# Attention, gated MLP and channel mixer on one core: VectorE's part of the last spatial weights in a step of its own, and the constants of the next stage behind the attention

## Chip, core and metric

The kernel runs on one core of a Trainium2 chip. The metric is the device time of one execution in microseconds (us); the median of three runs is given. Engines are named as the profile names them: PE (TensorE), DVE (VectorE), ACT (ScalarE), POOL (GpSimd), SP (SyncE, which only issues DMAs here).

## What is computed

Three layers follow one another; batch 8, 8 heads, 576 tokens, head size 64.

```python
# 1: attention with features (128 + 128 per token)
proj = q @ w_phi;  proj -= max(abs(proj));  phi = concat(exp(proj), exp(-proj))
kv = phi(k).T @ v;  z = phi(k).sum(tokens)
x  = (phi(q) @ kv) / (phi(q) @ z + 1e-6)
# 2: gated MLP over tokens
h = relu(x @ w_in);  u, v = halves(h)
v_n = (v - mean(v)) / sqrt(var(v) + 1e-6)
v_s = w_spatial @ v_n + b_spatial[:, None]
x = (u * v_s) @ w_out
# 3: low rank over tokens, then a channel MLP
u = x + V.T @ (U.T @ x);   out = u + relu(u @ w_ch1) @ w_ch2
```

Matmul operands of layers 2 and 3 are split into a high and a low part (`hi = round(w)`, `lo = w - hi`), and products use both.

## The kernel before

**Attention.** `attention` walks over 32 pairs of heads with a software pipeline, one period of the loop variable `p` for each (p from -1 to 34, the last ones draining). In period p PE projects the keys and queries of pair p+1 into one PSUM tile `pa` (line 402, tiles pk and pq), transposes the queries of p (pt, line 434), sums key times value of p and p+1 (pkv, lines 468 and 475), and makes the outputs of pairs p-2 and p-1 in four groups (pn, line 503), all with tag "pn" or "kv", one buffer each. DVE takes the largest value of a projection (mk and mq, line 411) and subtracts it (sk and sq, line 414); only then is `pa` free for the next projection. ACT makes the exponentials (kp, qp, e), POOL the low part of qp (line 456, two instructions for each e). An output group leaves PSUM by a copy to `nd`: on ACT (line 514), or on DVE for group 1 (line 512), and until that copy is done PE can't start the next group in the same buffer. These instructions are pinned: they keep the order in which the code writes them.

**Side work.** Between them `step(work)` runs one step of a side job at four places of a period: behind the subtraction sk ("slot 1"), behind kp ("slot 2"), between qp and e ("slot 3"), and at the period's end ("slot 4", called with `last=True`), ahead of the DVE copy `nd` of group 1. A step marked `late` runs at slot 4 alone. `with self.behind()` puts a step behind the latest pinned instruction of each engine. A job fetches weights, repacks and splits them; the next job begins when the last one is done. Side jobs share one staging buffer, tag "w32". The jobs in order: 16 pieces of `w_in`, four `w_sp` (rows of the spatial weights), `w_sp_tail` (the last 64 rows, and the bias in the free rows of the same tile `wt1`), 8 pieces of `w_out` (half a piece of 512 columns each; `raw_wo`, `bits_wo`, `w32_wo`), each four slots long. In `w_sp_tail` the step `bias` copies the 64 rows on ACT (line 212), subtracts on DVE (line 213), clears the staging tile for the bias on DVE (line 217) and issues its two DMAs on SP (line 220); the step `bias_split` makes two copies on ACT (line 228) and a subtraction on DVE (line 229). Both steps are late.

**Next stage.** `alloc_moe` (lines 636 to 651) runs once behind the attention's code: it allocates the tiles of layer 2 and writes the rows of constants for the bias, `vn1`, over a staging tile `pad` (DVE, lines 648 to 651). These instructions aren't pinned, and the scheduler of the framework may move them to an earlier place on their engine. Then `values(0, t)` for five tiles of tokens, t = 0 to 4: PE makes pv, ACT (DVE for the last) puts relu into v, DVE makes mean and variance (`bn_stats`, `bn_aggr`, lines 731 and 732), POOL the power -0.5 (rstd, line 734), DVE normalizes (line 739) and casts to vn0, POOL subtracts for vn1 (line 135). The normalization of tile t is written behind the statistics' matmuls of t+1. `gate(0)` follows: pu (two passes for each of four column blocks), then pz. PE's PSUM tiles have four buffers, so pu of the second block waits until the pv tile of t = 4 has been read (line 725). Meanwhile the attention's last divisions (x, POOL line 549, behind a DMA `rec`) are still under way.

Of the kernel before, what the change touches and what calls it, by code (L numbers as in the profile page):

```python
# [93 lines left out]
class Mixer:  # L94
# [69 lines left out]
    def weight_jobs(self):  # L164


        nc, jobs = self.nc, []
        S, R, NF, tail = self.S, self.R, self.NF, self.tail
# [34 lines left out]
        def w_sp_tail():  # L203


            wt0, wt1 = self.wt[0][:, NF, :], self.wt[1][:, NF, :]
            w = self.stage("wt", S)
            for i in range(2):
                nc.sync.dma_start(w[i * tail : (i + 1) * tail, :], self.w_spT[NF * P :, :])

            def bias():
                nc.scalar.copy(wt0, w)
                nc.vector.tensor_tensor(
                    out=wt1[:tail, :], in0=w[:tail, :], in1=wt0[:tail, :], op=ALU.subtract
                )
                b = self.stage("bs", S)
                nc.vector.memset(b[tail:, :], 0.0)
                for i in range(2):
                    r = tail + i * 32
                    nc.sync.dma_start(b[r : r + 1, :], self.b_sp)  # L220
                f = lambda: bias_split(b)
                f.late = True
                return f

            def bias_split(b):
                for i in range(2):
                    r = slice(tail + i * 32, tail + (i + 1) * 32)
                    nc.scalar.copy(wt1[r, :], b[r, :])
                nc.vector.tensor_tensor(
                    out=wt1[r, :], in0=b[r, :], in1=wt1[r, :], op=ALU.subtract  # L230
                )

            bias.late = True
            return bias

        jobs.append(w_sp_tail)
        def w_out(kk, h):
            def f():
# [397 lines left out]
    def alloc_moe(self, left, right):  # L636
        tc, nc, NF, tail = self.tc, self.nc, self.NF, self.tail
        self.ps = self.ctx.enter_context(
            tc.tile_pool(name="ps", bufs=1, space=PSUM, reuse_waits="tile")
        )  # L640
        mp = self.mp = left.enter_context(tc.tile_pool(name="mp", bufs=1, reuse_waits="tile"))
        self.gs = self.gated(0)
        mq = self.mq = right.enter_context(tc.tile_pool(name="mq", bufs=1, side="right", reuse_waits="tile"))


        self.vn = [mq.tile([P, self.NST, self.DH], F32R, name=f"vn{i}") for i in range(2)]
        pad = self.stage("pad", self.DH)
        nc.vector.memset(pad[tail:, :], 0.0)
        for r in (tail, tail + 32):
            nc.vector.memset(pad[r : r + 1, :], 1.0)  # L650
        nc.vector.tensor_copy(self.vn[1][tail:, NF, :], pad[tail:, :])

    def gated(self, b):
        return self.mp.tile([P, 2, self.KH, self.S], F32R, tag="g", name=f"g_{b}", bufs=1)
# [448 lines left out]
```

## Time and profile before

| | us |
|---|---|
| median of 3 runs | 1706.85 (1704.88 to 1708.28) |
| the profiled execution | 1698.59 |
| its span, first to last instruction | 1696.8 |
| what lies around the span | 1.8 |
| PE busy in the span | 1649.7 (97%) |
| attention, up to the first matmul of values(0, 0) | 387.9 |

A row of the timeline reads: start in us, length in us, engine, line, operation, output<-input, shapes, count of instructions merged into the row, and in brackets the idle time of the engine just before it and who ended it. A table by windows has one row for each stretch.

### The profile page before, as it was taken

How to read it: one execution, taken by the hardware profiler on the slowest of the kernel's cores; microseconds unless marked ns; L12 is line 12 of the kernel's file. 1: busy time of each engine (PE TensorE's matmuls, PEld its weight loads, DVE VectorE, ACT ScalarE, POOL GpSimd, SP SyncE). 2: the span in 40 equal slices, each digit the busy share in tenths (PEclk: the TensorE clock that was granted, in tenths of full speed). 3: DMA queues.
4: the chain of work that ended last, by engine and by line, in shares of the span. 5: the costliest groups of instructions: out<-in, count | busy, mean ns of one | idle time of the engine just before them, and what ended most of it. 6: DMA issues, size and time to landing. Idle time of an engine off the chain costs nothing.

```text
span 1696.8 us, 26606 instructions
## 1 busy us (share of the span) xinstructions
PE 1649.7 (97%) x10824; PEld 1559.9 (92%) x10824; DVE 741.5 (44%) x1234; ACT 609.4 (36%) x1092; POOL 470.4 (28%) x402
## 2 busy tenths in 40 slices
PE   7999989989999999999999999999999999999999
PEld 7998978978889789889789999999999999999999
DVE  6888766855656766656647112112111021121120
ACT  5888757863344443344334012011021120110110
POOL 3777775755333334224221000000000000000000
PEclk9999999999999999999999999999999999999999
DMA  4677665742233342232235101101001011011000
GB/s 136 196 199 212 203 189 145 197 124 71 79 121 98 117 122 87 91 109 82 70 101 164 38 1 37 38 1 38 21 18 38 1 38 38 1 38 38 1 19 20
DMA packets 86143, 141.42 MB, mean 83 GB/s; under 512 B 18626, under 2 KB 41314, under 8 KB 86020
## 3 DMA queue, kind: packets, MB, share of 16 engines
q1 hardware_dynamic: 85876, 139.65, 27.7%
q8 instruction: 85, 1.39, 0.3%
q14 instruction: 38, 0.31, 0.1%
q10 hardware_dynamic: 144, 0.07, 0.0%
HBM read 93.25 MB, written 36.85 MB: 77 GB/s over the span
## 4 chain that ended last, share of the span: by engine, by line
PE 78%; DMA 9%; DVE 4%; ACT 4%; issue 2%; POOL 2%; SPq 1%; DVEq 0%; POOLq 0%; ACTq 0%
PE pc L662 24%; PE ph L662 23%; DMA raw_c<-in_w_ch 5%; PE pu L662 4%; PE pn L503 4%; PE pv L662 4%; PE pkv L475 4%; PE px L662 4%; PE pz L662 2%; PE pk L402 1%; PE pt L434 1%; PE pt L867 1%; PE pq L402 1%; PE py L871 1%; DMA den<-nd 1%
## 5 line engine op out<-in xcount | busy, mean ns | idle before, releaser
L662 PE MATMUL pc<-h,w 128*128 128x384 f32 x2304 | 403.8, 336 | 0.0
L662 PEld LDWEIGHTS pc<-h,w 128*128 128x128 f32 x2304 | 402.0, 188 | 0.0
L662 PE MATMUL ph<-us,w 128*128 128x384 f32 x2244 | 391.0, 334 | 0.0
L662 PEld LDWEIGHTS ph<-us,w 128*128 128x128 f32 x2244 | 389.2, 188 | 0.0
L915 ACT ACTIVATE h<-ph 128x384 fp32r<-128x384 f32 x187 | 92.0, 492 | 628.5 <-PE ph L662 626.2
L135 POOL TENSOR_TENSOR us<-u,us 128x384 fp32r<-128x384 f32 x48 | 48.6, 1041 | 682.9 <-ACT us L132 673.9
L916 DVE SCALAR_TENSOR_TENSOR h<-ph,h 128x384 fp32r<-128x384 f32 x187 | 104.3, 558 | 273.1 <-ACT h L915 273.0
L503 PE MATMUL pn<-qp,kv 128*65 128x288 f32 x768 | 210.8, 335 | 13.0 <-DVE nd L512 9.7
L456 POOL TENSOR_TENSOR qp<-e,qp 128x576 fp32r<-128x576 f32 x128 | 184.1, 1460 | 132.3 <-ACT e L453 102.2
L951 DVE TENSOR_TENSOR u<-pc,u 128x384 f32<-128x384 f32 x48 | 25.7, 558 | 363.4 <-PE pc L662 363.4
L475 PE MATMUL pkv<-v,kp 128*128 128x65 f32 x1024 | 156.2, 256 | 0.0
L475 PEld LDWEIGHTS pkv<-v,kp 128*128 128x128 f32 x1024 | 155.4, 196 | 0.0
L503 PEld LDWEIGHTS pn<-qp,kv 128*65 128x65 f32 x768 | 101.4, 143 | 19.3 <-DVE nd L512 11.7
L662 PE MATMUL pz<-wt,vn 128*128 128x288 f32 x768 | 112.2, 295 | 0.0
L662 PEld LDWEIGHTS pu<-xs,wi 128*128 128x128 f32 x768 | 104.3, 191 | 3.2 <-DVE v L725 2.5
L662 PE MATMUL pu<-xs,wi 128*128 128x288 f32 x768 | 104.9, 298 | 2.3 <-DVE v L725 2.3
L662 PEld LDWEIGHTS pz<-wt,vn 128*128 128x128 f32 x768 | 105.3, 188 | 0.3 <-DVE u L808 0.3
L662 PE MATMUL px<-wo,g 128*128 128x512 f32 x384 | 93.9, 403 | 10.5 <-ACT g L132 10.5
L662 PEld LDWEIGHTS px<-wo,g 128*128 128x128 f32 x384 | 73.1, 194 | 29.0 <-ACT g L132 13.2
L662 PE MATMUL pv<-wi,xs 128*128 128x512 f32 x384 | 92.2, 394 | 0.0
L662 PEld LDWEIGHTS pv<-wi,xs 128*128 128x128 f32 x384 | 72.0, 188 | 15.6
L425 ACT ACTIVATE kp<-sk 128x1152 f32<-128x1152 f32 x64 | 74.4, 1164 | 31.2 <-DVE sk L414 23.4
(141 smaller groups left out, 1937.6 us busy)
## 6 DMA issues: line engine op xcount, KB each, us to landing
raw_c<-in_w_ch SPq DMA_DIRECT2D x32, 512.0 KB, 4.3
v<-in_v SPq DMA_DIRECT2D x32, 325.0 KB, 4.3
k<-in_kT SPq DMA_DIRECT2D x32, 320.0 KB, 3.7
q<-in_qT SPq DMA_DIRECT2D x32, 320.0 KB, 4.0
x<-nd SPq DMA_DIRECT2D x64, 144.0 KB, 3.3
rec<-rd SPq DMA_DIRECT2D x64, 144.0 KB, 3.3
xd<-x SPq DMA_DIRECT2D x32, 288.0 KB, 2.4
x<-xd SPq DMA_DIRECT2D x32, 288.0 KB, 3.1
```

Of the source, the lines that this page charges most:

```text
L135: return (nc.gpsimd if elo == "pool" else nc.vector).tensor_tensor(out=lo, in0=src, in1=hi, op=ALU.subtract)
L402: self.pin(nc.tensor.matmul(pa[:, j * NF + t, :], x[d, t * P : (t + 1) * P], ws[d, :], start=True, stop=True,))
L425: self.pin(self.nc.scalar.activation(kp, self.st[p]["sk"], AF.Exp, scale=1.0 - 2.0 * i))
L434: self.pin(nc.tensor.transpose(pt[:, at, :], s[:, u, :], self.ident))
L456: self.pin(nc.gpsimd.tensor_tensor(out=lo[:, c], in0=e[:, c], in1=hi[:, c], op=ALU.subtract))
L475: self.pin(nc.tensor.matmul(pkv[:, i, j, :], kp[:, j * NF + t, :], vb[:, u * D1 : (u + 1) * D1], start=False, stop=(j == 1 and t == NF - 1),))
L503: self.pin(nc.tensor.matmul(pn, kv[k][:, i, g // 2, :], qp[q][:, i, g * HS : (g + 1) * HS], start=(m == 0), stop=(m == len(terms) - 1),))
L662: self.nc.tensor.matmul(out, x, y, start=(start and i == 0), stop=(stop and i == len(terms) - 1))
L867: nc.tensor.transpose(pt[:, s0 - c0 : s0 - c0 + n], ts[t][0][:n, fs], self.ident[:n, :n])
L915: nc.scalar.activation(h[:, 0, :], ph, AF.Relu)
L916: nc.vector.scalar_tensor_tensor(out=h[:, 1, :], in0=ph, scalar=0.0, in1=h[:, 0, :], op0=ALU.max, op1=ALU.subtract,)
L951: nc.vector.tensor_tensor(out=u[:, f, :], in0=pcs[f], in1=u[:, f, :], op=ALU.add)
```

## The change

The job `w_sp_tail` gets two more steps. What was one step (ACT copy and DVE work) is now two: the ACT copies stay at slot 4, as late steps, and the DVE subtraction stands in a step of its own, which isn't late, so that it comes at slot 1 of the following period. The clearing of the bias's staging tile and its two DMAs go with the first of these subtractions. The job is one period longer by that, and all eight `w_out` jobs behind it begin one period later. In `alloc_moe` the four instructions for `pad` and the cast to `vn1` are put behind the attention's pinned instructions.

```diff
+            def late(f):
+                f.late = True
+                return f
+
             def bias():
                 nc.scalar.copy(wt0, w)
+                return less
+
+            def less():
                 nc.vector.tensor_tensor(
                     out=wt1[:tail, :], in0=w[:tail, :], in1=wt0[:tail, :], op=ALU.subtract
                 )
...
-                f = lambda: bias_split(b)
-                f.late = True
-                return f
-
-            def bias_split(b):
+                return late(lambda: bias_parts(b))
+
+            def bias_parts(b):
                 for i in range(2):
                     r = slice(tail + i * 32, tail + (i + 1) * 32)
                     nc.scalar.copy(wt1[r, :], b[r, :])
+                return lambda: bias_less(b, r)
+
+            def bias_less(b, r):
                 nc.vector.tensor_tensor(
                     out=wt1[r, :], in0=b[r, :], in1=wt1[r, :], op=ALU.subtract
                 )
...
-        nc.vector.memset(pad[tail:, :], 0.0)
-        for r in (tail, tail + 32):
-            nc.vector.memset(pad[r : r + 1, :], 1.0)
-        nc.vector.tensor_copy(self.vn[1][tail:, NF, :], pad[tail:, :])
+        with self.behind():
+            nc.vector.memset(pad[tail:, :], 0.0)
+            for r in (tail, tail + 32):
+                nc.vector.memset(pad[r : r + 1, :], 1.0)
+            nc.vector.tensor_copy(self.vn[1][tail:, NF, :], pad[tail:, :])
```

**Place 1: DVE at the end of period 20.** Names carry the pair of heads (sq21 belongs to pair 21); `wt1<-w32_wt,wt0` is the subtraction, `w32_bs` the staging tile of the bias. Before:

```order
L414 TENSOR_TENSOR sq21_3005<-pq21_2983,mq21_3004 128x1152
L213 TENSOR_TENSOR wt1_118<-w32_wt_2916,wt0_117 64x576
L217 MEMSET w32_bs_3043 64x576
L512 TENSOR_SCALAR nd19_3008<-pn19_1_3024,eps_133 65x288
L535 RECIPROCAL den9_18_2974<-den9_18_2974 128x9
L411 TENSOR_REDUCE mk22_3078<-pk22_3055 128x9
```

The same place now:

```order
L422 TENSOR_TENSOR sq21_3005<-pq21_2983,mq21_3004 128x1152
L520 TENSOR_SCALAR nd19_3008<-pn19_1_3024,eps_133 65x288
L543 RECIPROCAL den9_18_2974<-den9_18_2974 128x9
L419 TENSOR_REDUCE mk22_3073<-pk22_3050 128x9
L422 TENSOR_TENSOR sk22_3074<-pk22_3050,mk22_3073 128x1152
L220 TENSOR_TENSOR wt1_118<-w32_wt_2916,wt0_117 64x576
L224 MEMSET w32_bs_3079 64x576
L497 TENSOR_TENSOR kv1_21_3114<-pkv21_3011,kv0_21_3113 128x260
```

The subtraction and the clearing have moved from ahead of nd19 to behind sk22. The subtraction of the bias, line 229, moves in the same way, from ahead of nd20 to behind sk23.

**Place 2: DVE in period 30.** Before:

```order
L411 TENSOR_REDUCE mk31_4335<-pk31_4312 128x9
L648 MEMSET w32_pad_4604 64x512
L414 TENSOR_TENSOR sk31_4336<-pk31_4312,mk31_4335 128x1152
L650 MEMSET w32_pad_4604 1x512 x2
L489 TENSOR_TENSOR kv1_30_4369<-pkv30_4273,kv0_30_4368 128x260
```

Now:

```order
L419 TENSOR_REDUCE mk31_4325<-pk31_4302 128x9
L422 TENSOR_TENSOR sk31_4326<-pk31_4302,mk31_4325 128x1152
L60 TENSOR_SCALAR bits_wo3_1_4354<-raw_wo3_1_4300 128x256
L64 SCALAR_TENSOR_TENSOR bits_wo3_1_4354<-raw_wo3_1_4300,bits_wo3_1_4354 128x256
L68 ISA bits_wo3_1_4354<-bits_wo3_1_4354,low_wo3_1_4330 128x512
L497 TENSOR_TENSOR kv1_30_4365<-pkv30_4260,kv0_30_4364 128x260
```

The clearing of `pad` has left the place ahead of sk31, and the last piece of w_out stands in period 30 instead.

**Place 3: DVE and POOL at the first tile of layer 2's values.** st, mv and rstd are the statistics, v0_0 and v0_1 the tiles t = 0 and 1. DVE now (before, the rows of w32_pad, the cast to vn1 and w32_z stood above the first row, and the cast to vn0 ahead of the second BN_STATS):

```order
L740 BN_STATS st0_0_4627<-v0_0_4610 128x6
L543 RECIPROCAL den9_31_4575<-den9_31_4575 128x9
L657 MEMSET w32_pad_4604 64x512
L741 BN_AGGR mv0_0_4628<-st0_0_4627 128x2
L659 MEMSET w32_pad_4604 1x512 x2
L742 TENSOR_SCALAR rstd0_0_4629<-mv0_0_4628 128x1
L660 CAST vn1_4603<-w32_pad_4604 64x512
L748 TENSOR_SCALAR v0_0_4610<-v0_0_4610,mv0_0_4628,rstd0_0_4629 128x512
L740 BN_STATS st0_1_4652<-v0_1_4635 128x6
L134 CAST vn0_4602<-v0_0_4610 128x512
L741 BN_AGGR mv0_1_4653<-st0_1_4652 128x2
L269 MEMSET w32_z_4766 128x128
```

The constants have moved in between the statistics of t = 0 and their normalization, and each of the first two casts to vn0 behind the next tile's BN_STATS. POOL before:

```order
L734 TENSOR_TENSOR rstd0_0_4629<-rstd0_0_4629,mhalf_105 128x1
L135 TENSOR_TENSOR vn1_4603<-v0_0_4610,vn0_4602 128x512
L549 TENSOR_TENSOR x30_4532<-x30_4532,rec30_4556 128x576
L734 TENSOR_TENSOR rstd0_1_4654<-rstd0_1_4654,mhalf_105 128x1
L135 TENSOR_TENSOR vn1_4603<-v0_1_4635,vn0_4602 128x512
```

POOL now:

```order
L743 TENSOR_TENSOR rstd0_0_4629<-rstd0_0_4629,mhalf_105 128x1
L557 TENSOR_TENSOR x30_4532<-x30_4532,rec30_4556 128x576
L135 TENSOR_TENSOR vn1_4603<-v0_0_4610,vn0_4602 128x512
L743 TENSOR_TENSOR rstd0_1_4654<-rstd0_1_4654,mhalf_105 128x1
L135 TENSOR_TENSOR vn1_4603<-v0_1_4635,vn0_4602 128x512
```

On POOL the division x30, which waits for a DMA, has moved ahead of the first subtraction for vn1.

## Rows read from the trace of the kernel before

**Rows 1.** The page, part 1: busy us (share of span), instructions.
```profile
PE 1649.7 (97%) x10824; PEld 1559.9 (92%) x10824; DVE 741.5 (44%) x1234; ACT 609.4 (36%) x1092; POOL 470.4 (28%) x402
```

**Rows 2.** Timeline of DVE, 200 to 300 us (columns as told above).
```profile
236.93 1.30 DVE L411 TENSOR_REDUCE mk<-pk 128x9 f32<-128x1152 f32 x1
...
241.90 0.43 DVE L489 TENSOR_TENSOR kv<-pkv,kv 128x260 fp32r<-128x260 f32 x1 [2.21 <-ACT kv L488]
...
248.15 1.96 DVE L213 TENSOR_TENSOR wt<-w_wt,wt 64x576 fp32r<-64x576 f32 x1 [2.78 <-ACT wt L212]
250.34 0.54 DVE L217 MEMSET w_bs<- 64x576 f32 x1 [0.23 <-DVE wt L213]
...
251.46 1.29 DVE L411 TENSOR_REDUCE mk<-pk 128x9 f32<-128x1152 f32 x1
...
265.35 1.14 DVE L229 TENSOR_TENSOR wt<-w_bs,wt 32x576 fp32r<-32x576 f32 x1 [3.61 <-ACT wt L228]
...
267.07 1.29 DVE L411 TENSOR_REDUCE mk<-pk 128x9 f32<-128x1152 f32 x1
...
280.65 1.36 DVE L411 TENSOR_REDUCE mk<-pk 128x9 f32<-128x1152 f32 x1 [0.88 <-PE pk L406]
```

**Rows 3.** Timeline of all engines, 246 to 252 us.
```profile
247.44 0.67 ACT L212 CAST wt<-w_wt 128x576 fp32r<-128x576 f32 x1
248.10 3.26 POOL L456 TENSOR_TENSOR qp<-e,qp 128x576 fp32r<-128x576 f32 x2
...
251.48 0.35 PE L503 MATMUL pn<-qp,kv 128*65 128x288 f32 x1 [3.93 <-DVE nd L512]
```

**Rows 4.** Timeline of all engines, 263 to 268 us.
```profile
267.09 0.50 PE L503 MATMUL pn<-qp,kv 128*65 128x288 f32 x1 [3.16 <-DVE nd L512]
```

**Rows 5.** Windows of 2 us: PE, PEld, DVE, ACT, POOL busy; granted clock; DMA; GB/s.
```profile
252.00:254.00 2.00, 2.00 (x14) 2.00 (x12) 1.97 (x2) 0.00 (x0) 0.00 (x0) 0.51 0.40 82
```

**Rows 6.** Timeline of all engines, 355 to 373 us.
```profile
356.71 1.36 DVE L411 TENSOR_REDUCE mk<-pk 128x9 f32<-128x1152 f32 x1 [0.88 <-PE pk L406]
...
361.22 0.48 DVE L648 MEMSET w_pad<- 64x512 f32 x1 [3.15 <-POOL wo L135]
...
363.20 1.16 PE L402 MATMUL pq<-wst,q 64*128 64x128 f32 x16 [2.37 <-issue]
```

**Rows 7.** Timeline of PE, 355 to 440 us.
```profile
355.10 1.16 PE L402 MATMUL pk<-wst,k 64*128 64x128 f32 x16
...
356.43 0.38 PE L503 MATMUL pn<-qp,kv 128*65 128x288 f32 x1
...
372.29 0.35 PE L503 MATMUL pn<-qp,kv 128*65 128x288 f32 x1 [0.61 <-DVE nd L512]
```

**Rows 8.** Timeline of all engines, 390 to 409 us.
```profile
394.50 0.69 DVE L731 BATCH_NORM_STATS2 st<-v 128x6 f32<-128x512 f32 x1
394.67 1.30 POOL L135 TENSOR_TENSOR vn<-v,vn 128x512 fp32r<-128x512 f32 x1 [1.12 <-DVE vn L134]
...
397.46 1.44 POOL L549 TENSOR_TENSOR x<-x,rec 128x576 f32<-128x576 f32 x1 [1.50 <-DMA rec<-rd]
...
399.45 0.55 DVE L739 TENSOR_SCALAR v<-v,mv,rstd 128x512 f32<-128x512 f32 x1 [3.85 <-POOL rstd L734]
...
408.02 1.23 PE L662 MATMUL pu<-xs,wi 128*128 128x288 f32 x7 [2.27 <-DVE v L725]
```

**Rows 9.** Windows of 2 us, columns as in group 5.
```profile
366.00:368.00 2.00, 2.00 (x12) 1.98 (x12) 1.97 (x2) 1.05 (x2) 0.88 (x1) 0.50 0.37 76
...
410.00:412.00 2.00, 2.00 (x10) 2.00 (x10) 1.24 (x4) 0.62 (x2) 0.57 (x2) 0.50 0.00 0
```

**Rows 10.** Timeline of all engines, 236 to 272 us.
```profile
241.00 1.16 PE L402 MATMUL pq<-wst,q 64*128 64x128 f32 x16
...
245.20 0.53 SPq L372 DMA_DIRECT2D q<-in_qT  x1
```

**Rows 11.** The page, part 6: DMA issues, KB each, median us to landing.
```profile
q<-in_qT SPq DMA_DIRECT2D x32, 320.0 KB, 4.0
```

## The prediction

> **What bounds the kernel now.** I read part 1 of the page first: PE is busy 97% of the span [rows 1], so an edit on another engine pays only where PE stands still or runs at half its clock because of it. Then the timeline of DVE by periods of the attention, then the stretches in which a period is long, with all engines, and last the windows with the granted clock. The mark of a period is the start of its mk. Seven periods, from 280.65 to 356.71, take 76.06 us, 10.87 each [rows 2, 6]; PE shows no wait worth a row in them, so 10.87 is the undisturbed length. Three periods ahead of them take 236.93 to 280.65 [rows 2], 43.72 us where 3 x 10.87 = 32.6 would do: **11.1 us too long**, just where the two DVE subtractions of the change stand. A further period, 30, is long where `pad` is cleared.
>
> In the first case ACT makes its copy only at 247.44, behind the last e of the period, and the subtraction waits for it, 2.78 us of idle DVE, then takes 1.96 and the clearing of the bias tile follows with 0.54 [rows 2, 3]. The copy `nd` of group 1 is queued behind both on DVE, and PE needs the buffer that `nd` empties: PE stands still for 3.93 us [rows 3]. In the next period the same happens with the bias (DVE waits 3.61, the subtraction takes 1.14), and PE stands still for 3.16 [rows 2, 4]. That is 7.1 us of the 11.1. The other 4.0 is clock: after the stop the granted clock is 0.51 at 252 to 254 [rows 5], which is the lower level, 1.2 GHz of 2.4, and PE is busy all through that window.
>
> In period 30 the scheduler has put the clearing of `pad` ahead of sk31. It waits 3.15 us for POOL's last subtraction of `w_out`, since both use the one staging buffer [rows 6]. The subtraction sk31 comes late, the PSUM tile `pa` isn't free, and PE's projection pq starts after 2.37 us of idle [rows 6]; then the clock is at 0.50 again [rows 9].
>
> **The change part by part.**
>
> *The two subtractions.* At slot 4 only ACT's copies are left (0.67 us for the first; the second step has two). Neither is new, and `nd` of group 1 is on DVE, no longer behind anything. On DVE the subtraction and the clearing now stand between sk and the split kv of the next period, where DVE was idle for 2.21 us until ACT had copied kv [rows 2]. ACT's result has been there for several us by then, so no wait goes with them. Their price at the old durations is 1.96 + 0.23 + 0.54 = 2.73 us [rows 2], 0.5 more than the idle time; kv could be late by that, and PE's next pkv with it. I charge 0.2, bounds 0 and 0.5. The second subtraction, 1.14, fits. Gain: 11.1 - 0.2.
>
> The row of 1.96 us is long because POOL's pair of subtractions starts 0.05 us ahead of it and takes 3.26 [rows 3]. The Trainium skill (SBUF — State Buffer, Who interferes with whom) says that a VectorE instruction with two SBUF inputs and a GpSimd instruction that reads SBUF take a shared port in turn, for whole instructions; the row looks like that. By this rule the subtraction in its new place meets only the end of such a pair and is shorter, and the sum would be better by the 0.2; by the row alone it stays as charged.
>
> *The shifted job.* `w_sp_tail` ends a period later, so each of the eight `w_out` pieces does too, and the last one fills period 30. The seven undisturbed periods carry such pieces already, so a period with one costs 10.87: nothing added, nothing won. Its DMAs (raw_wo on SP) move with it; the first load of layer 3's U is issued a period later, while its reader comes behind 408. The bias's two DMAs move on SP from ahead of rd to behind v, ahead of den, x and q; see the last rival.
>
> *`pad` in period 30.* PE's groups there begin at 356.43 and the next ones at 372.29: 15.86 us. An undisturbed period is 10.87, but no keys are left to project, which takes off the pk pass, 355.10 to 356.43 = 1.33 [rows 7]; and without that pass PE waits 0.61 for `nd` [rows 7], which stays. So 10.87 - 1.33 + 0.61 = 10.15 is what it should be, and 5.7 us go. Of these 2.37 are the stop, and most of the rest is the clock.
>
> *`pad` in the next stage.* Here something is given back. DVE's clearing, cast and the clearing of z, some 2 us in all, come between the statistics and the normalization of tile 0. That alone costs nothing: tile 1 couldn't be normalized before 399.45, after 3.85 us of idle DVE, because POOL's division x waits for its DMA until 397.46 and rstd is behind it [rows 8]. But the order on POOL changes: x30 now stands ahead of the subtraction for vn1, which takes 1.30 [rows 8] and was done while POOL waited for the DMA. Now it comes between x30 and rstd: +1.30. One tile on, BN_STATS (0.69) stands ahead of the cast for which POOL's subtraction waits [rows 8]: +0.69, as the chain goes back and forth between DVE and POOL with nothing to spare. Both end at the read of the last pv tile, for which PE already waits 2.27 us at 408.02 [rows 8]: **+2.0** there. The bounds: 0, if the DMA comes later than the chain, and 4.1, if after the longer stop the lower clock lasts as long as after period 30's (5.7 - 2.37 - 0.22, the small wait behind it, = 3.1) and not only the 2 us at 0.50, or 1.0 lost, that the windows show at 410 now [rows 9]: 2.0 + 2.1. For the clock I take 0.4.
>
> *Sum.* 11.1 - 0.2 + 5.7 - 2.0 - 0.4 = **14.2 us less**. The profiled execution, 1698.59 with 1.8 around its span, would become 1684.4. It lies 8.3 below the median of the runs, which the trace doesn't explain; I take the same difference off the median: 1706.85 - 14.2 = 1692.6.
>
> **The rivals.**
>
> *More is given back.* PE waits the 0.5 us in period 21 and loses clock by it (4.0 for two stops, so 2.0 for one), and the values stage costs its upper 4.1. Then 16.8 - 2.5 - 4.1 = 10.2: 1696.6. For it: after each of the three stops shown the clock fell [rows 5, 9]. Against: 0.5 us is far shorter than these stops of 2.3 us and more, and kv needn't be late at all.
>
> *Nothing is given back.* The chain of the values ends with POOL's wait for the DMA of x31 anyway, or BN_STATS hides. Then 16.8, and 1.0 more if the clock holds: 1689.0 to 1690.0. Against: the DMA that POOL waited for had landed by 397.46, and both additions lie behind that [rows 8].
>
> *The stop moves instead of going.* The change may not do what it says, if what holds PE at the end of periods 20 and 21 is ACT's copies, not the DVE work behind them: they stay at slot 4. Then the 11.1 remain and only 5.7 - 2.4 = 3.3 go: 1703.5. Against: the bracket of PE's wait names nd on DVE both times [rows 3, 4], and ACT has nothing to do with that buffer.
>
> *Slower.* SP works in order, and the bias's DMAs, which wait for the clearing on DVE, now stand ahead of q, whose staging buffer is single. q is issued at 245.20, 8.27 into its period, and lands 4.0 later [rows 2, 10, 11]; the pq pass that reads it comes 10.87 + 4.07 = 14.94 in (241.00 is 4.07 in) [rows 10], so there is 2.7 us of slack. If the clearing were later than SP by more than that, PE would wait for q, with everything behind it. Subtraction and clearing can start when sk is done, 2.8 into the period (DVE falls idle 2.21 ahead of 241.90 [rows 2]), and be done at 2.8 + 2.73 = 5.5, and q itself is issued 8.27 in, so SP meets no wait; to be slower by 3.4 the hold has to be 2.7 + 14.2 + 3.4 = 20 us, nearly two periods, at one place: 1710.
>
> **How the numbers follow.** My forecast, 11 to 16.5 us less, gets 0.70; more given back 0.13; nothing given back 0.08; the stop that moves 0.06; slower 0.03. The likeliest gives 1692.6. The range takes in the first two rivals with half a microsecond to two for the scatter of the runs (they spread 1.7 around the median), and leaves out the last two: 1687.5 to 1698.0. A measurement of this kernel can tell about 0.2%, 3.4 us, from no change. Faster by more: 0.70 + 0.13 + 0.08 and a little of the fourth, 0.92; within: 0.05; slower: 0.03.
>
> **What would show it.** In the timeline of the changed kernel: mk to mk near 10.87 in periods 20 to 22, no PE wait for nd of 3 us, and a clock of 1.0 through them; the subtraction of the 64 rows directly behind sk, with no idle ahead of it; in period 30 sk31 behind mk31 at once and pq without a wait; at pu in the values stage a PE wait of about 4.3 us on line 734's read of the last pv tile, where it was 2.27. I am wrong if PE's waits in periods 20 to 22 are only renamed, if a new wait for kv or q stands in period 21, or if PE's wait in the values stage is above 7 us.

## The result and the profile after

The changed kernel takes 1689.26 us (median of 6 runs, 1685.94 to 1693.13); the kernel before, in runs beside it, 1705.87 (6 runs, 1695.98 to 1716.75). The ratio is 0.9912, interval 0.9886 to 0.9937: 0.9% faster, 15 us. A second set, with 17 runs of the kernel before, gave 0.9899 (0.9874 to 0.9924). The prediction was 1692.6 in a range of 1687.5 to 1698.0.

The profiled execution of the changed kernel has a span of 1686.3, 10.5 below that of before. To see where it went I cut the spans at five marks: the start of the mk of period 20, three periods on, the mk of period 30, the first pv matmul of layer 2 and the first pz matmul. All numbers are differences of start times in the timelines; the last row ends with the span. A 0 stands where the prediction has no term.

| stretch, us | before | changed | changed, 2nd profile | predicted change |
|---|---|---|---|---|
| start to mk of period 20 | 236.9 | 240.2 | 244.0 | 0 |
| periods 20 to 22 | 43.7 | 32.6 | 32.6 | -10.9 |
| periods 23 to 29 | 76.1 | 76.6 | 76.3 | 0 |
| mk of period 30 to first pv | 31.2 | 25.5 | 25.3 | -5.7 |
| first pv to first pz | 29.7 | 32.5 | 31.5 | +2.4 |
| first pz to the end | 1279.2 | 1279.0 | 1278.1 | 0 |

The three periods first: DVE's timeline of the changed kernel, the rows that answer to [rows 2]. DVE instructions in order of time; start, length, idle time ahead in brackets.

```profile
251.81 1.30 DVE L419 TENSOR_REDUCE mk<-pk 128x9 f32<-128x1152 f32 x1
253.22 1.36 DVE L422 TENSOR_TENSOR sk<-pk,mk 128x1152 f32<-128x1152 f32 x1
254.49 0.74 DVE L220 TENSOR_TENSOR wt<-w_wt,wt 64x576 fp32r<-64x576 f32 x1
255.47 0.54 DVE L224 MEMSET w_bs<- 64x576 f32 x1 [0.23 <-PE pn L511]
256.45 0.43 DVE L497 TENSOR_TENSOR kv<-pkv,kv 128x260 fp32r<-128x260 f32 x1 [0.45 <-ACT kv L496]
...
262.08 1.36 DVE L419 TENSOR_REDUCE mk<-pk 128x9 f32<-128x1152 f32 x1 [0.33 <-PE pk L414]
...
264.93 1.14 DVE L237 TENSOR_TENSOR wt<-w_bs,wt 32x576 fp32r<-32x576 f32 x1
267.04 0.43 DVE L497 TENSOR_TENSOR kv<-pkv,kv 128x260 fp32r<-128x260 f32 x1 [0.96 <-ACT kv L496]
...
272.72 1.36 DVE L419 TENSOR_REDUCE mk<-pk 128x9 f32<-128x1152 f32 x1 [0.88 <-PE pk L414]
```

Both subtractions start as soon as sk is done, with no idle time in their brackets, and kv still waits a little for ACT behind them: nothing is late by them. The two PE waits of 3.93 and 3.16 us [rows 3, 4] have no row any more, and the granted clock is 1.00 in every window of 2 us from 238 to 276 us. The first subtraction takes 0.74 us, where it took 1.96 beside POOL's pair [rows 3]; in this kernel that pair is over at 254.36 us, 0.13 ahead of it.

Period 30, on the timelines of DVE and PE, the rows that answer to [rows 6]:

```profile
349.34 1.36 DVE L419 TENSOR_REDUCE mk<-pk 128x9 f32<-128x1152 f32 x1 [0.88 <-PE pk L414]
350.80 1.36 DVE L422 TENSOR_TENSOR sk<-pk,mk 128x1152 f32<-128x1152 f32 x1
```

```profile
353.40 1.16 PE L410 MATMUL pq<-wst,q 64*128 64x128 f32 x16
```

sk31 follows mk31 at once, and pq starts without a wait.

What was given back stands at the first tile of the values. Timeline of POOL, changed kernel, the rows that answer to [rows 8]:

```profile
381.78 0.70 POOL L743 TENSOR_TENSOR rstd<-rstd,mhalf 128x1 f32<-128x1 f32 x1 [1.87 <-DVE rstd L742]
384.29 1.43 POOL L557 TENSOR_TENSOR x<-x,rec 128x576 f32<-128x576 f32 x1 [1.81 <-DMA rec<-rd]
385.67 1.30 POOL L135 TENSOR_TENSOR vn<-v,vn 128x512 fp32r<-128x512 f32 x1
386.93 0.56 POOL L743 TENSOR_TENSOR rstd<-rstd,mhalf 128x1 f32<-128x1 f32 x1
389.08 1.29 POOL L135 TENSOR_TENSOR vn<-v,vn 128x512 fp32r<-128x512 f32 x1 [1.59 <-DVE vn L134]
```

The subtraction for vn1 (1.30) now stands between x and the rstd of the second tile. The end of that chain, PE's wait for the read of the last pv tile, and the clock behind it (windows of 2 us; the column ahead of the DMA share is the granted clock):

```profile
396.53 1.81 PE L671 MATMUL pu<-xs,wi 128*128 128x288 f32 x6 [3.92 <-DVE v L734]
```

```profile
394.00:396.00 2.00, 0.00 (x0) 0.00 (x0) 1.97 (x3) 0.00 (x0) 1.18 (x2) 0.94 0.00 1
396.00:398.00 2.00, 1.47 (x6) 1.47 (x7) 1.93 (x3) 0.00 (x0) 1.24 (x1) 0.50 0.37 146
398.00:400.00 2.00, 2.00 (x10) 2.00 (x9) 1.18 (x5) 0.18 (x1) 0.54 (x1) 0.50 0.00 0
400.00:402.00 2.00, 2.00 (x11) 2.00 (x10) 1.97 (x4) 0.44 (x2) 1.33 (x1) 0.50 0.00 0
402.00:404.00 2.00, 2.00 (x15) 2.00 (x15) 0.81 (x3) 0.62 (x2) 0.00 (x0) 0.85 0.03 8
```

PE waits 3.92 us instead of 2.27, and the clock is at its lower level for some 6 us of PE's work behind it. In the second profile PE waits 4.14 us.

### The profile page after: what moved, and what is told of

It is laid out like the page before. It is cut to its first block, busy times and chain, and to the rows that moved or that the text cites. A ratio compares the mean times of both kernels' runs of the same rounds, so it can differ in the third digit from the quotient of the medians.

```text
span 1686.3 us, 26604 instructions
## 1 busy us (share of the span) xinstructions
PE 1643.5 (97%) x10824; PEld 1554.4 (92%) x10824; DVE 742.6 (44%) x1234; ACT 609.7 (36%) x1092; POOL 469.0 (28%) x402
## 4 chain that ended last, share of the span: by engine, by line
PE 79%; DMA 9%; ACT 4%; DVE 4%; POOL 2%; issue 2%; SPq 1%; POOLq 0%; ACTq 0%; DVEq 0%
PE pc L671 24%; PE ph L671 23%; DMA raw_c<-in_w_ch 5%; PE pn L511 4%; PE pu L671 4%; PE pv L671 4%; PE pkv L483 4%; PE px L671 4%; PE pk L410 2%; PE pz L671 2%; PE pt L442 1%; PE pt L876 1%; PE pq L410 1%; PE py L880 1%; DMA den<-nd 1%
## 5 line engine op out<-in xcount | busy, mean ns | idle before, releaser
L671 PE MATMUL px<-wo,g 128*128 128x512 f32 x384 | 93.6, 401 | 11.1 <-ACT g L132 11.1
```

The lines of the kernel that those rows point to most:

```text
L671: self.nc.tensor.matmul(out, x, y, start=(start and i == 0), stop=(stop and i == len(terms) - 1))
```

## The experiments

Where nothing else is said, the same five marks are compared. The kernel before ran beside each set: 1705.19 in the first (17 runs), 1706.95 in the second (11), 1704.28 in the third (11).

### The changed kernel again, and its two halves

First set, four kernels on one chip. The yardstick:

> The changed kernel once more, as the yardstick of this set. From the mk of period 20 to the first pu matmul behind PE's long wait in layer 2's values: 171.1 us in the profile before (236.93 to 408.02), 156.4 in the profile of the changed kernel (240.17 to 396.53). Every theory: 155 to 158 here, and 13 to 18 us off the time of the kernel before.

Measured: 1688.83 us; ratio 0.9899 (0.9874 to 0.9924). From the mk of period 20 to pu 156.1 us, PE's wait at pu 4.14. As expected.

The steps alone; the constants as they were (edit against the changed kernel):

```diff
-        with self.behind():
-            nc.vector.memset(pad[tail:, :], 0.0)
...
+        nc.vector.memset(pad[tail:, :], 0.0)
...
```

> The changed steps of the last spatial weights alone; the constants of the next stage are written as before, not behind the pinned instructions. With the w_out pieces one period later, the scheduler sets the clearing of pad into period 31, behind a reciprocal, and leaves x30 on POOL behind the first subtraction for vn1. Theory 1 (the stop of period 30 goes by the shift of the job alone, and putting the constants behind the attention only costs): the stretch from the mk of period 20 to pu takes 153 to 155 us, PE waits about 2.3 us ahead of pu instead of 3.9, and the time is 2 to 4 us below the changed kernel, 17 to 20 below the kernel before. Rival (the stop of period 30 went because the constants were moved): a DVE wait for POOL at pad comes back in period 30 or 31, the stretch takes 160 to 163 us, and the kernel is 4 to 6 us slower than the changed one. Second rival (the longer wait at pu comes with the run, not with the order): as the changed kernel within 1 us.

Measured: 1687.94 us; ratio 0.9889 (0.9862 to 0.9916). The stretch to pu takes 155.5, PE's wait at pu 2.45, from mk of period 30 to the first pv 25.4, from pv to pz 28.3 (32.5 and 31.5 in the changed kernel). DVE around `pad` in this kernel:

```profile
353.93 1.36 DVE L422 TENSOR_TENSOR sk<-pk,mk 128x1152 f32<-128x1152 f32 x1
355.20 1.07 DVE L60 TENSOR_SCALAR bits_wo<-raw_wo 128x256 int32<-128x256 int32 x1
```

```profile
362.19 0.20 DVE L543 RECIPROCAL den<-den 128x9 f32<-128x9 f32 x1
367.77 0.48 DVE L656 MEMSET w_pad<- 64x512 f32 x1 [5.38 <-POOL wo L135]
368.42 1.12 DVE L658 MEMSET w_pad<- 1x512 f32 x2 [0.17 <-PE pn L511]
369.57 0.43 DVE L497 TENSOR_TENSOR kv<-pkv,kv 128x260 fp32r<-128x260 f32 x1
```

The clearing of `pad` still waits for POOL, 5.38 us now, but in a draining period, where sk31 isn't behind it and no PE row shows a wait for it. So the longer job is enough for the stop of period 30 to go: it pushes the last piece of w_out, and with it the clearing, one period on. Putting the constants behind the attention isn't needed for it, and the stretch from pv to pz is 3 to 4 us longer with them there (1.5 of that hangs on the clock, see the last section). Theory 1 held in the trace, and the second rival falls by the wait at pu, 2.45 against 4.14. The whole time doesn't show it: 2 to 4 us below the changed kernel were expected, and the two are 0.9 us apart, with intervals that overlap.

The constants alone, with the steps of before (edit against the kernel before):

```diff
-        nc.vector.memset(pad[tail:, :], 0.0)
...
+        with self.behind():
+            nc.vector.memset(pad[tail:, :], 0.0)
...
```

> The constants behind the attention alone; the last spatial weights as before. Theory 1 (the parts are separate and add up): the three long periods stay, 43 to 45 us for three; period 30 is 5.7 us shorter; the wait at pu is 4 us rather than 2.3 and the clock after it costs 1 to 1.5 more, so the stretch takes 167 to 169 us and the time falls by 1 to 3.5 us against the kernel before. Rival (the period 30 stop is worth more than its own row): more than 5 us faster. Second rival (what the constants cost at pu eats it all): no faster than before.

Measured: 1702.74 us; ratio 0.9977 (0.9961 to 0.9994), 2.5 us off the median. Three periods 44.7, mk of period 30 to pv 26.3 (4.9 shorter), pv to pz 30.6 (0.9 longer), PE's wait at pu 3.24, where 4 was expected; the stretch to pu 169.7, 0.7 above the expected 167 to 169. Theory 1 held in the main: without the shift this half, too, takes the stop of period 30, and gives part of it back.

### Constants in a place of their own

A column of one element for each partition, not in the shared staging buffer:

```diff
-        pad = self.stage("pad", self.DH)
+        pad = self.sp.tile([P, 1], F32, tag="pad", name="pad", bufs=1)
...
-            nc.vector.tensor_copy(self.vn[1][tail:, NF, :], pad[tail:, :])
+        nc.vector.tensor_copy(
+            self.vn[1][tail:, NF, :], pad[tail:, :].to_broadcast([P - tail, self.DH])
+        )
```

> The changed steps, and the constants in a column of their own (one element for each partition, not in the shared staging buffer), cleared at the start of the kernel and spread by the cast to vn1; not behind the pinned instructions. Theory 1 (the shared buffer is what ties pad to POOL and the order on DVE): no wait at pad, x30 on POOL behind the first subtraction for vn1, PE's wait at pu about 2.3 us, the stretch 153 to 155 us, time as the steps alone within 1.5 us. Rival (some other work holds the values stage): PE's wait at pu is 3.5 us or more as in the changed kernel.

Measured: 1689.15 us; ratio 0.9903 (0.9878 to 0.9928). PE's wait at pu fell to 0.74 and pv to pz to 26.6, below the expectation, but the mk of period 30 to pv takes 29.2. Who waited for whom from 352 to 390 us, in us in total, times, longest:

```profile
DVE w_z L269 <- POOL wo L135: 5.3, 1, 5.3
...
PE pn L511 <- ACT nd L522: 4.1, 2, 3.1
...
ACT ua L271 <- DVE w_z L269: 3.1, 1, 3.1
```

With `pad` out of the staging buffer the next tile in it, z (zeros for layer 3's ua and ub), was scheduled earlier. It waits for POOL as `pad` did, ACT's copies of it wait for z, and they stand on ACT ahead of an `nd`: the stop of before, on another engine. Theory 1 was wrong on pu (0.74, not about 2.3) and on the stretch to pu (158.3 us, not 153 to 155). The two belong together: the stop delays the first pv and not the DMA for which x30 waits. x30 starts on POOL 7.95 us behind the first pv, where it was 9.70 in the steps alone; that is 1.75 us less, and PE's wait at pu is 1.71 shorter. The short wait is the other side of the stop and no merit of the column.

### One stop by itself

The steps alone, with the first subtraction back in ACT's late step (the edit that sets it apart from the steps alone):

```diff
                 nc.scalar.copy(wt0, w)
-                return less
-
-            def less():
```

> The steps alone with the first subtraction put back into the late step of ACT's copy: one of the two stops, by itself, at the end of period 20, and no other difference. Theory 1 (a stop costs its idle time and the clock behind it): PE waits 3 to 4 us for nd there, the three periods from the mk of period 20 take 38 to 40 us (33.8 with the steps alone, 32.6 in the changed kernel), the time is 4 to 7 us above the steps alone. Rival (the idle time is made up in the next periods, by work that PE has ahead): 35 us or less.

Measured: 1694.62 us; ratio 0.9938 (0.9917 to 0.9959), against 0.9889 of the steps alone, in another set: 0.5%, some 8 us, where 4 to 7 were expected. Three periods take 37.7, 3.9 more than the steps alone. Only that part belongs to the stop; in the profiles the mk of period 20 also comes 3.6 us later, periods 23 to 29 take 1.9 longer, and the clock at pu costs 1.5. The stop is back as it was, on the timeline of all engines and that of PE:

```profile
257.38 1.96 DVE L217 TENSOR_TENSOR wt<-w_wt,wt 64x576 fp32r<-64x576 f32 x1 [2.78 <-ACT wt L216]
259.58 0.54 DVE L221 MEMSET w_bs<- 64x576 f32 x1 [0.23 <-DVE wt L217]
260.15 0.51 DVE L517 TENSOR_SCALAR nd<-pn,eps 65x288 f32<-65x288 f32 x1
```

```profile
260.71 0.35 PE L508 MATMUL pn<-qp,kv 128*65 128x288 f32 x1 [3.93 <-DVE nd L517]
```

The rival, that the idle time would be made up, falls: it had 35 us or less. The figure is 0.3 below the expected 38 to 40. The 33.8 that it is compared with already holds a long period of 12.5, behind a PE wait of 2.74 us for `nd` at the end of the period ahead.

### What stands ahead of nd

The kernel before, with the place of `nd` at a period's end as the only change:

```diff
-            work = step(work, True)
             taken()
+            work = step(work, True)
```

> The kernel before, with nothing changed but the place of nd at a period's end: ahead of the side job's step. The subtractions of the last spatial weights keep their late step and still wait for ACT's copies. Theory 1 (nd queued behind the subtraction is the cause of both stops): PE's waits of 3.9 and 3.2 us for nd vanish; mk, which stands behind the subtraction, comes 2 to 3.5 us late instead, and PE does other work for 2 to 3 us of that, so that three periods take 34 to 39 us in place of 43.7; the time falls by 5 to 10 us against before. Rival (ACT's copies at that place are the cause): three periods stay above 42 us and the time within 2 us of before.

Measured: 1695.10 us; ratio 0.9938 (0.9918 to 0.9957), 11 us, where 5 to 10 were expected; three periods 36.0. DVE in the first of them, where the subtraction is still behind ACT's late copy, and PE's waits in the two periods behind it:

```profile
253.24 0.75 DVE L213 TENSOR_TENSOR wt<-w_wt,wt 64x576 fp32r<-64x576 f32 x1 [1.54 <-ACT wt L212]
254.22 0.54 DVE L217 MEMSET w_bs<- 64x576 f32 x1 [0.24 <-DVE wt L213]
```

```profile
257.71 1.16 PE L402 MATMUL pq<-wst,q 64*128 64x128 f32 x16 [0.90 <-PE pn L503]
...
270.74 1.16 PE L402 MATMUL pq<-wst,q 64*128 64x128 f32 x16 [1.44 <-issue]
```

The late ACT copies are all still there, and the waits of 3.9 and 3.2 us for `nd` are gone. So the rival of the prediction by which ACT's copies hold PE falls: it was DVE's work ahead of `nd`. What stays late is mk and sk. PE waits 0.9 and 1.4 us instead, and both times pq starts 0.1 us behind the end of sk, which frees the projection's buffer.

The same edit with the steps:

> The steps alone (constants as before the change), and at a period's end the copy nd of group 1 is issued ahead of the side job's step, no longer behind it. Theory 1 (what holds PE in these periods is any DVE work that stands ahead of nd and waits; the four casts of the spatial weights, which wait 0.9 to 3.2 us for their DMA, are such work, and they make the runs scatter): no PE wait for nd of over 1 us in periods 16 to 20; from the mk of period 16 to that of period 20 43 to 46 us (45.5 in before, 50.3 in the repeated changed kernel, 47.1 with the steps alone); the time 2 to 6 us below the steps alone. Rival (the wait goes over to the subtraction sk and the projection behind it, as the reciprocal and mk stand behind the cast): the periods keep their length, and the time stays within 1.5 us of the steps alone.

Measured: 1686.74 us; ratio 0.9884 (0.9869 to 0.9900). PE's waits for `nd` in periods 16 to 20 are gone, but the stretch takes 47.7 us, not 43 to 46: here theory 1 was wrong. DVE in that kernel:

```profile
226.17 0.51 DVE L520 TENSOR_SCALAR nd<-pn,eps 65x288 f32<-65x288 f32 x1 [1.04 <-PE pn L511]
228.77 0.60 DVE L134 CAST wt<-w_wt 128x576 fp32r<-128x576 f32 x1 [2.09 <-DMA w_wt<-in_w_spT]
229.87 0.22 DVE L543 RECIPROCAL den<-den 128x9 f32<-128x9 f32 x1 [0.49 <-DMA den<-nd]
230.00 1.30 DVE L419 TENSOR_REDUCE mk<-pk 128x9 f32<-128x1152 f32 x1
```

and PE behind it:

```profile
232.86 1.16 PE L410 MATMUL pq<-wst,q 64*128 64x128 f32 x16 [1.06 <-issue]
```

The cast waits 2.09 us for the DMA of the spatial weights; `nd` is ahead of it now, but mk is behind it, and the wait goes over to the projection: the rival. Against the steps alone nothing is settled (0.9884 to 0.9889).

### Where the wait at pu comes from

The changed kernel, with the constants later still, behind the last tile's normalization:

```diff
             self.normalize()
+            if b == 0 and f == 0:
+                self.constants()
             self.last[0] = act.ins
```

> The changed kernel with the constants written still later: behind the normalization of the last tile of values, ahead of the first pz matmuls that read them. Theory 1 (it is the place of the constants among the statistics of the first tile, and x30 ahead of the subtraction for vn1 on POOL, that makes PE wait longer at pu): the wait at pu is 2.3 to 2.7 us as with the steps alone, from the first pv to the first pz 28 to 30 us (32.5 and 31.5 in the two profiles of the changed kernel). Rival (the constants cost wherever they stand): 31 us or more, or a new wait of pz for vn1.

Measured: 1691.39 us; ratio 0.9920 (0.9891 to 0.9948). The wait at pu is 2.32 and pv to pz 30.3. Theory 1 held on the wait at pu: the place of the constants among the first tile's statistics is what lengthened it. The stretch is 0.3 above what it gave. The zeros z follow the constants in the staging buffer, and so come late, too; ACT's copies of them wait, and the first pz waits for ACT's u behind these copies:

```profile
400.11 0.30 ACT L271 CAST ua<-w_z 128x128 fp32r<-128x128 f32 x1 [4.33 <-DVE w_z L269]
```

```profile
402.57 1.86 PE L674 MATMUL pz<-wt,vn 128*128 128x288 f32 x12 [0.42 <-ACT u L799]
```

In the whole time this kernel can't be told from the changed one (0.9912 and 0.9899).

The steps alone, with the last two divisions (x30 and x31) on DVE:

```diff
-        self.pin(self.nc.gpsimd.tensor_tensor(out=x, in0=x, in1=rec, op=ALU.mult))
+        eng = self.nc.vector if p >= self.B * self.NP - 2 else self.nc.gpsimd
+        self.pin(eng.tensor_tensor(out=x, in0=x, in1=rec, op=ALU.mult))
```

> The steps alone, and the last two divisions (x30, x31) on DVE in place of POOL. Theory 1 (PE's wait at pu comes from rstd queued on POOL behind x30, which waits for its DMA): the wait falls from 2.4 to under 1 us if DVE can do x30 while it would wait itself, the stretch from the first pv to the first pz takes 26 to 28 us (28.3 with the steps alone). Rival (the wait goes with x30 to DVE, whose queue holds the normalization): the wait stays between 2 and 4 us.

Measured: 1687.34 us; ratio 0.9884 (0.9870 to 0.9899). From pv to pz 27.1, PE's wait at pu 1.19, between the two expectations. POOL's rstd no longer waits behind x30, but DVE does:

```profile
383.66 0.76 DVE L558 TENSOR_TENSOR x<-x,rec 128x576 f32<-128x576 f32 x1 [2.32 <-DMA rec<-rd]
...
384.85 0.56 POOL L743 TENSOR_TENSOR rstd<-rstd,mhalf 128x1 f32<-128x1 f32 x1 [2.74 <-DVE rstd L742]
```

So nearly all of the wait behind x30 goes with it to its new queue. Counted from the first pv, the second tile's normalization starts at 11.50 us, where it was 11.68 with the steps alone: 0.2 us won. The rest is won at the fourth tile, and by x31. With the steps alone its normalization runs beside x31 on POOL, and with x31 gone from POOL it is short:

```profile
395.28 1.40 POOL L557 TENSOR_TENSOR x<-x,rec 128x576 f32<-128x576 f32 x1
395.35 1.62 DVE L747 TENSOR_SCALAR v<-v,mv,rstd 128x512 f32<-128x512 f32 x1 [0.91 <-POOL rstd L742]
```

```profile
391.28 0.55 DVE L748 TENSOR_SCALAR v<-v,mv,rstd 128x512 f32<-128x512 f32 x1 [0.90 <-POOL rstd L743]
```

That is 1.07 of the 1.26 us by which the wait is shorter. The row takes 1.61 to 1.64 us in all ten profiles with x31 on POOL, and 0.55 in the two with x31 on DVE (this run and the next). Theory 1 had named the smaller cause. In the span the gain doesn't show: behind the first pz this profile takes 1285.3 us, 6.2 more than the steps alone, and why is open.

All three together, the steps, `nd` first and the divisions on DVE:

> All three: the steps, nd ahead of the side job's step, the last two divisions on DVE. Theory 1: the gains add, 3 to 7 us below the steps alone, 20 to 25 us below before. Rival: as the better one of the two parts.

Measured: 1682.29 us (5 runs, 1680.31 to 1688.93); ratio 0.9866 (0.9848 to 0.9885), 23 us below the kernel before. It lies 4.5 to 5 us below each of the two it is made of, run on the same chip, and some 7 below the changed kernel of the first two sets. That is within what theory 1 gave, but its interval still overlaps theirs, so the rival, no more than the better part, isn't ruled out. It has the lowest median of this study.

## Why the prediction was right, and where it wasn't

**Periods 20 to 22: right.** 11.1 was read as going, 0.2 charged; from 43.72 to 32.55 us, 11.2 are gone in both profiles of the changed kernel. The charge for a late kv wasn't needed: the subtraction took 0.74, not 1.96, and kv waited 0.45 us for ACT. In the second profile PE waits 0.35 us for kv in period 21, but there, too, kv itself waited 0.45 for ACT and not for the subtraction. The rule of the Trainium skill set beside the row in the prediction (SBUF — State Buffer, Who interferes with whom) was the better guide here. The traces agree with it: the subtraction takes 1.96 where POOL's pair starts just ahead of it (before, and one stop back), 1.21 where it meets the last 0.6 us of the pair (steps alone), 0.74 where the pair is over, and 0.75 where it starts 0.01 us ahead of the pair (the kernel before with `nd` first).

**That it was nd's place on DVE: right, and tested.** Taking `nd` ahead of the job's step in the kernel before, ACT's copies untouched, took both waits away; putting one subtraction back brought one wait of 3.93 us.

**Period 30: right in size, wrong in whose it is.** 5.7 predicted, 31.2 to 25.5 measured. But the prediction put the gain under the constants' new place and called the shifted job "nothing added, nothing won". The steps alone have 25.4 there, the constants alone 26.3: either half takes the stop by itself. The shift moves the last w_out piece, and the clearing that waits for it, into a period where the wait holds nobody. What failed is the order I looked at: that of the whole change, and not that of each half.

**The values stage: mechanism right, the clock not forecast.** PE's wait at pu was to grow from 2.27 to about 4.3; it is 3.92 and 4.14. The order on POOL and DVE was the cause: in the four kernels with the constants elsewhere, x30 on POOL and no stop in period 30 (steps alone, constants later, one stop back, steps with `nd` first) it is 2.3 to 2.7. The term for the clock was 0.4. The 60 pu matmuls behind the wait take 9.74 us in the kernel before, and 10.92 and 9.74 in the two profiles of the changed kernel, so the clock cost 1.2 more in one and nothing more in the other. The stretch from pv to pz grew by 2.8 and 1.8, around the 2.4 in all: 1.65 of wait and 1.2 of clock in the first, the wait alone in the second. The 0.4 lies between two outcomes; why the one or the other comes isn't shown. That the clock cost 1.0 before the change was read from one window; the matmuls say 1.5 (9.74 us against 8.21 in the steps alone, where the clock stayed at 1.00).

**What the prediction didn't see: the stretch ahead of the change.** In the profile of before the mk of period 20 starts at 236.9; in the eleven profiles taken later, at 237.3 to 246.2. Part of the difference, up to 4.4 us, lies ahead of the mk of period 16, and its cause is open. The other part, 0.2 to 4.8 us, lies in the periods of the four earlier rows of spatial weights, whose casts on DVE stand ahead of `nd` too (but for the kernels with `nd` first) and wait for a DMA that is not always there. In the second profile of the changed kernel, on DVE:

```profile
216.26 0.46 DVE L134 CAST wt<-w_wt 128x576 fp32r<-128x576 f32 x1 [3.22 <-DMA w_wt<-in_w_spT]
...
228.69 0.93 DVE L134 CAST wt<-w_wt 128x576 fp32r<-128x576 f32 x1 [2.81 <-DMA w_wt<-in_w_spT]
```

PE waits 1.65 and 2.05 us for `nd` there. In the profile of before the longest of these DVE waits was 1.51 us. The constants alone differ from before only in the place of `pad`, and their profile reaches the mk of period 20 at 244.8, 7.9 us later. So the profiled execution of before was a lucky one. This is likely a good part of the 8.3 us between it and the median that the prediction left open, and of why the profiles differ by 10.5 us and the medians by 16.6. That isn't shown: the runs without a profile can't be cut.

The forecast of 1692.6 is 3.3 above the measured median, within the scatter of the runs (7 us from lowest to highest); the sum of the terms, 14.2, stands against 15 by the ratio, and 13.5 and 15.0 in the two profiles from the mk of period 20 to the first pz (180.7 to 167.1 and 165.6). Of the rivals, "the stop moves" and "slower" are out: the waits for `nd` are gone, and q was never waited for. "Nothing is given back" is out too, with 2.8 and 1.8 us given back from pv to pz. "More is given back" wanted 2.5 us in period 21 and 4.1 at pu; neither came, only the first profile's clock leaned that way.

## What to carry to other kernels

When an engine takes its instructions in order, as DVE does in all these timelines, don't look only at what an instruction costs but at what is queued behind it while it waits: here 2 to 3 us of work that nobody hurried for held PE for 7 us and its clock for four more, because a 0.5 us copy stood behind it. A wait that can't be removed can be put where nothing urgent follows; a shared staging buffer passes such a wait on to whatever uses it next, so check its next user too. Look also at what runs on POOL beside a DVE instruction of the critical chain: here x31 made one row 1.07 us longer. When a change has two halves, look at the order that each half gives by itself before crediting one of them.

## What the runs showed that I had not expected

The clock after a wait of about 2.3 to 2.7 us at pu is not the same from profile to profile. In the lowest window of 2 us it was 0.50 after 2.27 us (before), 2.32 (constants later) and 2.68 (steps, nd first), and 0.57 after 2.41 (one stop back); it stayed at 1.00 after 2.45 (steps alone) and 2.64 (before, nd first). After the shorter waits of this study (0.74 to 1.34, three profiles) it stayed, after the longer ones (3.24 to 4.14, three profiles) it fell. The 60 pu matmuls behind it take 9.7 us in the first case and 8.2 in the second, so 1.5 us hang on it. In the steps alone, windows of 2 us with the clock ahead of the DMA share:

```profile
396.00:398.00 2.00, 0.00 (x0) 0.00 (x0) 1.97 (x3) 0.13 (x1) 1.18 (x2) 1.00 0.22 89
398.00:400.00 2.00, 1.93 (x14) 1.93 (x15) 1.88 (x4) 0.04 (x1) 0.77 (x1) 1.00 0.15 59
400.00:402.00 2.00, 2.00 (x17) 2.00 (x16) 1.23 (x4) 0.57 (x2) 0.54 (x1) 1.00 0.00 0
```

PE stands still through the whole first window, and the clock stays. What the steps alone gained from pv to pz (28.3 against 29.7 in the kernel before, at nearly the same wait) is this luck and no merit of the order; with the lower clock they would stand at 29.8 by estimate (28.3 + 1.5), still 1.7 to 2.7 below the changed kernel.
